# Zero rows for the 64-row operands of block attention on TensorE

## The chip, the cores and the metric

The kernel runs on one core of a Trainium2 chip. The metric is the device time of one execution in microseconds (us); less is better. Engines: TensorE (PE, with its weight loads PEld), VectorE (DVE), ScalarE (ACT), GpSimd (POOL) and the queue engine SyncE (SP).

## What is computed

Block-causal attention over 4 batches of 8 heads (576 tokens, head size 64), a mixture of experts (top 2 of 8) on the result, and a dense MLP behind it. The change lies in the attention:

```python
block = 64
scores = scale * np.matmul(q, k.transpose(0, 1, 3, 2))
pos = np.arange(S)                                   # S = 576
mask = (pos[:, None] // block) >= (pos[None, :] // block)
scores = np.where(mask, scores, -1000000000.0)
scores = scores - np.max(scores, axis=-1, keepdims=True)
attn = np.exp(scores)
attn = attn / (np.sum(attn, axis=-1, keepdims=True) + 1e-09)
return np.matmul(attn, v)                            # D = 64
```

`x = attention`, then `x = moe(x)` with 512 -> 1024 -> 512 per expert, then `mlp(x)` with 512 -> 2048 -> 512, all in float32.

## The kernel before

The program has three stretches: attention with the gating of each batch (to about 280 us), the experts, and the dense MLP.

Attention works head by head, 32 heads, a pair of heads per load. The 576 queries are cut into five chunks `QC`: the first has 64 queries, the others 128. The keys are cut from the other end: four chunks of 128 keys and a last one of 64. So a query chunk sees whole key blocks, chunk c sees 64 + 128c keys, and the mask falls into the last 64 keys of a chunk only. Numbers that need more than one pass of the array's precision are split in a high and a low part (`pth`, `ptl`; the V tile holds its high and low part side by side, 2 x 64 columns).

For each head and chunk these steps run:

- `scores` (L726): PE writes Q K^T into a PSUM tile `sb`; it works by units (0 and 1 together, 2, 3, 4).
- `rowmax` (L740) on DVE with a memset of the masked corner (L927), then `expo` (L747) on ACT, which writes P[c], one SBUF tile per query chunk with (c + 1) x 128 columns, and the row sums `rs`.
- `ptrans` (L765): PE transposes P[c] in pieces of 128 keys into a PSUM bank `tb`. P[0] has 64 rows, so its transpose takes 64 rows and a 64 x 64 piece of the identity. The piece (0, 1) is left out.
- `pt_hi` (L593, on ACT or DVE) and `pt_lo` (L784, DVE) write the transposed P into `pth` and `ptl`: key chunk kc at column kc x 576, keys on the partitions. Key chunk 4 has 64 keys and so fills 64 partitions, and only query chunk 4 (128 columns) sees it.
- `av` (L800): PE multiplies V with `pth` and `ptl`. Part 0 covers queries 0 to 319 with key chunks 0 to 2, part 1 queries 320 to 575 with key chunks 0 to 4. Where fewer than 256 columns remain, the product with `ptl` takes the 64 high columns of V alone. For key chunk 4 only the `nk` = 64 rows that exist are passed.
- `av_out`, `fin` (L822, PE: projects back to tokens and adds the gate's weights), `x_out` (DVE), `lsum` (POOL).

In the transposes P is the stationary operand (the weights) and the identity moves through; in the V products V is stationary and P moves.

The order of each engine's instructions comes from a planner (`Plan`): every operation gets a cost per engine, its dependencies, a priority and a PSUM bank, and is placed when engine, operands and bank would be free. The planned costs stand in the calls of `add`; the engines then run these fixed orders and wait for each other by semaphores. The constants of the phase are filled by POOL ahead of the loop (L613 to L626): zero rows of the raw inputs, the columns of P behind the visible keys, ones in `rs`. The V tile's rows 64 to 127 of key chunk 4 are zero from there.

Of the kernel before, what the change touches and what calls it, by code (L numbers as in the profile page):

```python
# [7 lines left out]
F32 = mybir.dt.float32  # L8
# [7 lines left out]
PSUM = bass.MemoryType.PSUM  # L16
# [20 lines left out]


class Bank:
    """A PSUM bank of a pool, held from the op that takes it until every op that drops it is done."""  # L40

    def __init__(self, pool, least):
        self.pool, self.least, self.left, self.bank, self.tile = pool, least, 0, None, None


class Plan:
    """Static list scheduling: each op is emitted when its engine, its operands and a PSUM bank would be free."""

    LAT = {"PE": 0.26, "DVE": 0.17, "ACT": 0.17, "POOL": 0.15, "SP": 2.0}
    OWN = {"PE": 0.0, "DVE": 0.13, "ACT": 0.13, "POOL": 0.1, "SP": 0.0}  # L50
# [81 lines left out]
def kernel(  # L132
# [14 lines left out]
    nc = tc.nc  # L147
    B, H, S, D = q.shape
# [24 lines left out]
    y_tab = tc.dram_tile([E * CAP + OVF * 128, DM], F32, name="y_tab")  # L173
# [24 lines left out]
    ident = const.tile([128, 128], F32, name="ident")  # L198
# [70 lines left out]
    slot = [const.tile([128, B, NC], I32, name=f"slot{i}") for i in range(2)]  # L269
# [137 lines left out]
        nc.vector.scalar_tensor_tensor(h[1][:, c0:c1], ps[:, :c1 - c0], 0.0, h[0][:, c0:c1].bitcast(F32),  # L407
                                       op0=OP.max, op1=OP.subtract)

# [1 line left out]
    gctx = ExitStack()  # L411
    sqk_p = gctx.enter_context(tc.tile_pool(name="sqk", bufs=2, side="right", reuse_waits="tile"))
    g_p = gctx.enter_context(tc.tile_pool(name="g", bufs=1, side="right", reuse_waits="tile"))
# [159 lines left out]
    with actx:  # L573
        pool = lambda name, bufs: actx.enter_context(tc.tile_pool(name=name, bufs=bufs))
# [11 lines left out]
        PW = S  # L586
# [23 lines left out]
        def dve(n):  # L610
            return {"DVE": 0.07 + n / 960.0}

        # constants of this phase  # L613
        for nm, pad in (("q", 0), ("k", NC - 1), ("v", NC - 1)):
            for i in range(2):
                if i or nm == "v":
# [1 line left out]
        P = []  # L618
        for c in range(NC):
            P.append(one.tile([128, (c + 1) * 128], F32, name=f"P{c}"))  # L620
            nc.gpsimd.memset(P[c][:, c * 128 + 64:], 0.0)
        rs = []
        for i in range(3):
            rs.append(one.tile([128, NC], F32, name=f"rs{i}"))
            nc.gpsimd.memset(rs[i][64:, 0:1], 1.0)
        pth = one.tile([128, 4 * PW + S], F32R, name="pth")  # L626
        ptl = one.tile([128, 4 * PW + S], F32R, name="ptl")

        def init_iw(e):
            for r in range(2):  # L630
                rows = slice(r * 64, (r + 1) * 64)
                for i, wo in enumerate((0, D)):
                    for j, src in enumerate((w_gate, w_noise)):
                        nc.sync.dma_start(iw[rows, :, i, wo + j * E:wo + (j + 1) * E],
                                          src.rearrange("(j i d) e -> i d j e", d=D, i=2)[i])
# [120 lines left out]
        def ptrans(g, i):  # L756
            ps = tb[g.bank]
            q0, n = PTQ[i]
            for c, kc in PT[i]:
                if (c, kc) == (0, 1):  # L760
                    continue
                s0, m = QC[c]
                o = (kc - PTK[i][0]) * n + s0 - q0
                nk = min(128, S - kc * 128)
                nc.tensor.transpose(ps[:nk, o:o + m], P[c][:m, kc * 128:kc * 128 + nk], ident[:m, :m])  # L765

        def pslice(t, i):
            k0, k1 = PTK[i]
# [20 lines left out]
        def av(g, hd, part):  # L789
            c0, c1 = PARTS[part]  # L790
            a, n = PQ[part]
            z = a + n
            vs = sp["v", hd // 2]
            o = tb[g.bank]
            for kc in range(c1):
                nk = min(128, S - 128 * kc)
                q0 = max(a, QC[kc][0])
                for ti, pp in enumerate((pth, ptl) if kc < c1 - 1 else (ptl, pth)):
                    w = D if pp is ptl and z - q0 < 256 else 2 * D
                    nc.tensor.matmul(o[:w, q0 - a:z - a], lhsT=vs[:nk, kc, hd % 2, :w],  # L800
                                     rhs=pp[:nk, kc * PW + q0:kc * PW + z],
                                     start=(kc == 0 and ti == 0), stop=(kc == c1 - 1 and ti == 1))

        def av_out(e, g, hd, part):
# [52 lines left out]
        for p in range(NPAIR):  # L857
            b, j = pairs[p]
            u0 = 2 * NU * p
            # operands of the pair  # L860
            for n_, nm in enumerate("qkv"):
                if p or nm == "v":
                    k["L", nm, p] = add({"SP": 1.6}, lambda e, p=p, nm=nm: load(p, nm),
# [49 lines left out]
            for hd in (2 * p, 2 * p + 1):  # L913
                i_ = hd % 2
                h = hd % H
                last = hd == HD - 1
# [82 lines left out]
            add({"DVE": 0.34}, lambda e, f=f, g=g: h_lo(hT["a", f], tb[g.bank], 0, AHEAD * 128), [hh], PR["es"] + f, drop=g)  # L999
        busy = plan.run({"POOL": 4.4, "DVE": 2.9, "PE": 4.4 + 0.216 * WARM0, "ACT": 2.0, "SP": 3.7})  # L1000

# [1 line left out]
    work = ctx.enter_context(tc.tile_pool(name="work", bufs=2, reuse_waits="tile"))  # L1003
    ps_h = ctx.enter_context(tc.tile_pool(name="ps_h", bufs=2, space=PSUM, reuse_waits="tile"))
    ps_y = ctx.enter_context(tc.tile_pool(name="ps_y", bufs=1, space=PSUM, reuse_waits="tile"))
# [74 lines left out]
    ovf = {}  # L1080

    def route_rows():
        """Rows of y_tab by token, and the list of slot tiles past the main capacity."""
        R = [128, 2 * NC, E]
        cps = ps_x.tile([128, E], F32, tag="x", name="cps")
        nc.tensor.matmul(cps, lhsT=ones, rhs=ohsum[B - 1], start=True, stop=True)
        cnt = work.tile([128, E], F32, tag="cnt", name="cnt", bufs=1)
        nc.vector.tensor_copy(cnt, cps)
        yield
        ge = work.tile([128, E, NV], F32, tag="ge", name="ge", bufs=1)  # L1090
        nc.vector.tensor_tensor(ge, cnt[:, :, None].to_broadcast([128, E, NV]),
                                tstart[:, None, :].to_broadcast([128, E, NV]), op=OP.is_gt)
        yield
        nt = work.tile([128, E], F32, tag="nt", name="nt", bufs=1)
        nc.vector.tensor_reduce(nt, ge, axis=AX.X, op=OP.add)
        yield
        cum = work.tile([128, E], F32, tag="cum", name="cum", bufs=1)
        nc.vector.tensor_tensor_scan(cum, one8, nt, 0.0, op0=OP.mult, op1=OP.add)
        yield
        off = work.tile([128, E], F32, tag="off", name="off", bufs=1)  # L1100
        nc.vector.tensor_tensor(off, cum, nt, op=OP.subtract)
        yield
        nc.vector.tensor_scalar(off, off, 128.0, float(E * CAP - MAIN), op0=OP.mult, op1=OP.add)
        yield
        nc.vector.tensor_tensor(off, off, erow, op=OP.subtract)
        yield
        for b in range(B):
            t = work.tile([128, 2 * NC, E], F32, tag="rt", name="rt", bufs=1)
            oh = ohs[b].rearrange("p i c e -> p (i c) e")
            pf = posi[b].rearrange("p i c -> p (i c)")  # L1110
            m = work.tile([128, 2, 2 * NC], F32, tag="rm", name="rm")
            for r, row in enumerate((erow, off)):
                nc.vector.tensor_tensor(t, oh, row[:, None, :].to_broadcast(R), op=OP.mult)
                yield
                nc.vector.tensor_reduce(m[:, r], t, axis=AX.X, op=OP.add)
                yield
            nc.vector.scalar_tensor_tensor(m[:, 1], pf, float(MAIN), m[:, 1], op0=OP.is_ge, op1=OP.mult)
            yield
            nc.vector.tensor_tensor(m[:, 0], m[:, 0], pf, op=OP.add)
            yield  # L1120
            nc.vector.tensor_tensor(m[:, 0], m[:, 0], m[:, 1], op=OP.add)
            yield
            for i in range(2):
                nc.vector.tensor_copy(slot[i][:, b], m[:, 0, i * NC:(i + 1) * NC])
                yield
        L = [128, OVF, E]
        le = work.tile([128, OVF, E], F32, tag="le", name="le", bufs=1)
        nc.vector.tensor_tensor(le, cum[:, None, :].to_broadcast(L), ovn[:, :, None].to_broadcast(L), op=OP.is_le)
        yield
        lst = const.tile([128, 2, OVF], F32, name="lst")  # L1130
        nc.vector.tensor_reduce(lst[:, 0], le, axis=AX.X, op=OP.add)
        yield
        nc.vector.tensor_tensor(le, le, nt[:, None, :].to_broadcast(L), op=OP.mult)
        yield
        nc.vector.tensor_reduce(lst[:, 1], le, axis=AX.X, op=OP.add)
        yield
        nc.vector.tensor_tensor(lst[:, 1], ovn, lst[:, 1], op=OP.subtract)
        yield
        nc.vector.tensor_scalar(lst[:, 1], lst[:, 1], 128.0, float(MAIN), op0=OP.mult, op1=OP.add)
        yield  # L1140
        nov = const.tile([128, 1 + OVF], I32, name="nov")
        nc.vector.tensor_copy(nov[:, 0:1], cum[:, E - 1:E])
        nc.vector.tensor_copy(nov[:, 1:], lst[:, 0])
        for i in range(2):
            for r in range(2):
                rows = slice(r * 64, (r + 1) * 64)
                nc.vector.tensor_copy(srd[i][rows], slot[i][0:64].rearrange("p (a r) c -> p r a c", r=2)[:, r, :, 0])
                nc.vector.tensor_copy(rrd[i][rows], rw[i][0:64].rearrange("p (a r) c -> p r a c", r=2)[:, r, :, 0])
                yield
        ovf["lst"], ovf["nov"] = lst, nov  # L1150
        yield 0
# [87 lines left out]
    def combined(gi, t):  # L1239
        x_tile(("m", gi), gath.pop((gi, t))[0][0], t, len(GR[gi]) * 128)  # L1240

    # the first tiles of expert 0 while the last tokens are routed
    plan2 = Plan({"h": 2, "x": 1, "y": NT - AHEAD})
    add = plan2.add
    k2 = {}
# [53 lines left out]
    wraw2[0] = ctx.enter_context(tc.tile_pool(name="wraw2", bufs=4, side="right", reuse_waits="tile"))  # L1299

    rr = route_rows()
    NG = len(STEPS)
    conv_at = [g for g in range(7, NG) if g % 3][:32]
# [40 lines left out]
        if NG - NF + 5 <= g < NG - NF + 5 + len(GR[0]):  # L1344
            combined(0, g - (NG - NF + 5))

# [1 line left out]
    def m_s1(i, gi, f):  # L1348
        n = len(GR[gi]) * 128
        ps = s1(("m", gi), f, U0 + i, 0, n, SP0 if gi == 0 else ())  # L1350
# [73 lines left out]
```

## Time and profile before

| | us |
|---|---|
| median of 3 runs | 1156.43 |
| range of the runs | 1153.89 to 1157.19 |
| profiled execution, span from its first to its last instruction | 1155.9 |
| PE busy in it | 1137.4 |
| DVE busy | 802.6 |
| ACT busy | 567.7 |
| POOL busy | 280.7 |

The page gives no other time for the profiled execution than its span; it lies 0.5 us below the median of the runs. In the timeline each row has a start, a length, engine, line, operation, tiles, and for PE the active rows and columns of the array as "rows*columns" ahead of the output's shape (partitions x elements). Equal neighbours are merged to one row with a count (x7), and the shape shown is that of the first. A matmul's recorded length holds its whole way through the array, so neighbours overlap; the distance of two starts tells what one operation took from PE. A group "rows*columns" of 64*128 is an operand with 64 rows.

### The profile page before, as it was taken

How to read it: one execution, taken by the hardware profiler on the slowest of the kernel's cores; microseconds unless marked ns; L12 is line 12 of the kernel's file. 1: busy time of each engine (PE TensorE's matmuls, PEld its weight loads, DVE VectorE, ACT ScalarE, POOL GpSimd, SP SyncE). 2: the span in 40 equal slices, each digit the busy share in tenths (PEclk: the TensorE clock that was granted, in tenths of full speed). 3: DMA queues.
4: the chain of work that ended last, by engine and by line, in shares of the span. 5: the costliest groups of instructions: out<-in, count | busy, mean ns of one | idle time of the engine just before them, and what ended most of it. 6: DMA issues, size and time to landing. Idle time of an engine off the chain costs nothing. (4 is left out here: it accounts for less than half of the span.)

```text
span 1155.9 us, 18249 instructions
## 1 busy us (share of the span) xinstructions
PE 1137.4 (98%) x6652; PEld 991.3 (86%) x6652; DVE 802.6 (69%) x1659; ACT 567.7 (49%) x1179; POOL 280.7 (24%) x299
## 2 busy tenths in 40 slices
PE   7999999999999999999999999899999999999998
PEld 5888889888898999999999999798888888888887
DVE  7888888888658878878778774577555564554543
ACT  5788787885443333333323233466444344443442
POOL 5545635443720101010100000176320230200000
PEclk9999999999999999999999999999999999999999
DMA  6754565221296785865564531522110110100000
GB/s 136 192 140 114 130 152 124 53 63 40 94 387 222 248 286 179 278 243 185 176 229 156 205 111 37 184 82 70 31 46 23 42 47 0 56 1 1 37 1 37
DMA packets 134340, 139.71 MB, mean 121 GB/s; under 512 B 67816, under 2 KB 97512, under 8 KB 134248
## 3 DMA queue, kind: packets, MB, share of 16 engines
q1 hardware_dynamic: 118568, 100.30, 27.6%
q0 software_dynamic: 8480, 28.78, 9.0%
q10 hardware_dynamic: 7200, 9.44, 2.3%
q8 instruction: 53, 0.87, 0.3%
q14 instruction: 39, 0.32, 0.1%
HBM read 92.94 MB, written 36.70 MB: 112 GB/s over the span
## 5 line engine op out<-in xcount | busy, mean ns | idle before, releaser
L381 PE MATMUL h<-xh,wah 128*128 128x312 f32 (+5 forms) x832 | 279.9, 336 | 2.9 <-DVE hl L407 2.8
L383 PE MATMUL h<-xh,wal 128*128 128x312 f32 (+5 forms) x832 | 275.1, 331 | 0.0
L382 PE MATMUL h<-xl,wah 128*128 128x312 f32 (+5 forms) x832 | 275.0, 331 | 0.0
L1060 PE MATMUL y<-wbh,hh 128*128 128x512 f32 (+1 forms) x608 | 238.2, 392 | 2.1 <-issue 2.1
L1061 PE MATMUL y<-wbl,hh 128*128 128x512 f32 (+1 forms) x608 | 238.7, 393 | 0.2
L1062 PE MATMUL y<-wbh,hl 128*128 128x512 f32 (+1 forms) x608 | 237.7, 391 | 0.0
L381 PEld LDWEIGHTS h<-xh,wah 128*128 128x128 f32 x832 | 157.6, 189 | 15.2 <-DVE hl L407 3.2
L382 PEld LDWEIGHTS h<-xl,wah 128*128 128x128 f32 x832 | 157.7, 190 | 11.5
L383 PEld LDWEIGHTS h<-xh,wal 128*128 128x128 f32 x832 | 157.4, 189 | 10.3
L1062 PEld LDWEIGHTS y<-wbh,hl 128*128 128x128 f32 (+1 forms) x608 | 113.7, 187 | 25.8
L1060 PEld LDWEIGHTS y<-wbh,hh 128*128 128x128 f32 (+1 forms) x608 | 113.8, 187 | 23.5 <-issue 2.6
L1061 PEld LDWEIGHTS y<-wbl,hh 128*128 128x128 f32 (+1 forms) x608 | 113.8, 187 | 22.3 <-POOL wbl L331 0.8
L404 ACT ACTIVATE hh<-h 128x312 fp32r<-128x312 f32 (+4 forms) x128 | 55.2, 431 | 145.7 <-PE h L383 144.2
L1353 DVE SCALAR_TENSOR_TENSOR r<-r,h 128x512 f32<-128x512 f32 (+1 forms) x80 | 50.5, 631 | 109.1 <-ACT r L1352 108.8
L1352 ACT ACTIVATE r<-h,three 128x512 f32<-128x512 f32 (+1 forms) x80 | 51.6, 645 | 126.9 <-PE h L383 126.7
L1224 POOL DMA_INDIRECT ga<-y_tab,slot x32 | 37.9, 1185 | 295.0 <-DMA wb<-w_out 114.4
L331 DVE TENSOR_TENSOR wal<-wa,wah 128x1024 fp32r<-128x1024 f32 x75 | 93.2, 1243 | 16.6 <-ACT wah L327 16.3
L1038 POOL DMA_INDIRECT xn<-x_tok,ids x38 | 38.9, 1024 | 269.4 <-PE xps L344 264.9
L747 ACT ACTIVATE P<-sb,nm 128x320 f32<-128x320 f32 (+4 forms) x160 | 84.8, 531 | 22.1 <-DVE nm L740 18.8
L331 DVE TENSOR_TENSOR wbl<-wb,wbh 128x1024 fp32r<-128x1024 f32 x71 | 86.5, 1218 | 12.9 <-ACT wbh L327 12.9
L347 ACT CAST xh<-xps 128x512 fp32r<-128x512 f32 x56 | 32.6, 586 | 126.7 <-PE xps L344 126.7
L1356 DVE TENSOR_TENSOR hl<-r,hh 128x512 fp32r<-128x512 f32 (+1 forms) x80 | 56.3, 703 | 51.5 <-ACT hh L1355 51.0
(236 smaller groups left out, 1990.2 us busy)
## 6 DMA issues: line engine op xcount, KB each, us to landing
wa<-in_moe_w_dram SPq DMA_DIRECT2D x23, 512.0 KB, 5.3
wb<-in_moe_w_dram SPq DMA_DIRECT2D x23, 512.0 KB, 8.5
qw<-qk POOLq DMA_DIRECT2D x30, 288.0 KB, 3.4
y_tab<-yo SPq DMA_DIRECT2D x32, 256.0 KB, 4.1
w<-in_moe_w_in_dram SPq DMA_DIRECT2D x16, 512.0 KB, 6.7
y_tab<-zero SPq DMA_DIRECT2D x8, 1024.0 KB, 9.9
w<-in_moe_w_out_dram SPq DMA_DIRECT2D x16, 512.0 KB, 5.6
wa<-in_moe_w_dram ACTq DMA_DIRECT2D x9, 512.0 KB, 9.5
```

The source lines that it names most:

```text
L331: (nc.gpsimd if e == "POOL" else nc.vector).tensor_tensor(lo, raws[PS[u]][which], hi.bitcast(F32), op=OP.subtract)
L381: nc.tensor.matmul(ps, lhsT=wh, rhs=xh, start=first, stop=False)
L382: nc.tensor.matmul(ps, lhsT=wh, rhs=xl, start=False, stop=False)
L383: nc.tensor.matmul(ps, lhsT=wl, rhs=xh, start=False, stop=last)
L404: nc.scalar.activation(h[0][:, c0:c1], ps[:, :c1 - c0], AF.Relu)
L747: nc.scalar.activation(o, views.pop((hd, c)), AF.Exp, bias=nms.pop((hd, c))[:n], scale=1.0, accum_out=rs[hd % 3][:n, c:c + 1])
L1060: nc.tensor.matmul(yps[t][:n], lhsT=hh[:, sl], rhs=wh[:, f % 2], start=first, stop=False)
L1061: nc.tensor.matmul(yps[t][:n], lhsT=hh[:, sl], rhs=wl[:, f % 2], start=False, stop=False)
L1062: nc.tensor.matmul(yps[t][:n], lhsT=hl[:, sl], rhs=wh[:, f % 2], start=False, stop=last)
L1352: nc.scalar.activation(r[:, :n], ps[:, :n], AF.Relu, bias=three, scale=1.0)
L1353: nc.vector.scalar_tensor_tensor(r[:, :n], r[:, :n], 6.0, ps[:, :n], op0=OP.min, op1=OP.mult)
L1356: nc.vector.tensor_tensor(hl[:, :n], r[:, :n], hh[:, :n].bitcast(F32), op=OP.subtract)
```

## The change

Three edits, all in attention. The transpose of P[0] is made with 128 rows and 128 moving columns (`ptrans`); for this P[0] is filled with zeros as a whole. The V products of key chunk 4 take 128 rows of `pth`, `ptl` and V; for this rows 64 to 127 of the last 128 columns of `pth` and `ptl` are filled with zeros once.

```diff
         for c in range(NC):
             P.append(one.tile([128, (c + 1) * 128], F32, name=f"P{c}"))
-            nc.gpsimd.memset(P[c][:, c * 128 + 64:], 0.0)
+            nc.gpsimd.memset(P[c] if c == 0 else P[c][:, c * 128 + 64:], 0.0)
...
         pth = one.tile([128, 4 * PW + S], F32R, name="pth")
         ptl = one.tile([128, 4 * PW + S], F32R, name="ptl")
+        for t in (pth, ptl):
+            nc.gpsimd.memset(t[64:, 4 * PW + S - 128:].bitcast(F32), 0.0)
...
                 nk = min(128, S - kc * 128)
-                nc.tensor.transpose(ps[:nk, o:o + m], P[c][:m, kc * 128:kc * 128 + nk], ident[:m, :m])
+                nc.tensor.transpose(ps[:nk, o:o + 128], P[c][:, kc * 128:kc * 128 + nk], ident)
...
             for kc in range(c1):
-                nk = min(128, S - 128 * kc)
                 q0 = max(a, QC[kc][0])
...
-                    nc.tensor.matmul(o[:w, q0 - a:z - a], lhsT=vs[:nk, kc, hd % 2, :w],
-                                     rhs=pp[:nk, kc * PW + q0:kc * PW + z],
+                    nc.tensor.matmul(o[:w, q0 - a:z - a], lhsT=vs[:, kc, hd % 2, :w],
+                                     rhs=pp[:, kc * PW + q0:kc * PW + z],
```

The rest of the diff takes comments and docstrings away. The planner's costs are as they were, so the order of instructions is the same on every engine but POOL, which has two more fills at the start. Line numbers behind the edits are 1 or 2 higher.

PE, one head in the middle of attention, around the transpose of P[0] (L765 before, L767 after; the shapes are those of the output). Before:

```order
L726 MATMUL sb_182<-qk 128x320
L726 MATMUL sb_182<-qk,qw 128x320
L765 MATMUL tb_176<-ident,P_187 128x64
L765 MATMUL tb_176<-ident,P_189 128x128 x2
L765 MATMUL tb_180<-ident,P_195 128x128 x4
```

And after:

```order
L728 MATMUL sb_182<-qk,qw 128x320
L767 MATMUL tb_176<-ident,P_187 128x128
L767 MATMUL tb_176<-ident,P_189 128x128 x2
L767 MATMUL tb_180<-ident,P_195 128x128 x4
L801 MATMUL tb_178<-pth,sp_v 128x256
```

Nothing has moved; the first transpose writes 128 columns instead of 64, of which the next one overwrites the upper 64.

POOL at its start, from the fill of P[0] to the first low part of V. Before:

```order
L621 MEMSET P_187 128x64
L621 MEMSET P_189 128x64
L621 MEMSET P_191 128x64
L621 MEMSET P_193 128x64
L621 MEMSET P_195 128x64
L625 MEMSET rs_197 64x1
L625 MEMSET rs_199 64x1
L625 MEMSET rs_201 64x1
L651 TENSOR_TENSOR sp_v<-raw_v_76,sp_v 128x10x64
```

And after:

```order
L621 MEMSET P_187 128x128
L621 MEMSET P_189 128x64
L621 MEMSET P_191 128x64
L621 MEMSET P_193 128x64
L621 MEMSET P_195 128x64
L625 MEMSET rs_197 64x1
L625 MEMSET rs_199 64x1
L625 MEMSET rs_201 64x1
L629 MEMSET pth 64x128
L629 MEMSET ptl 64x128
L653 TENSOR_TENSOR sp_v<-raw_v_76,sp_v 128x10x64
```

Two fills stand between the last `rs` and the first split, and the fill of P[0] is twice as wide. ACT's first exponential of a 64 x 64 tile waits for POOL in the new program, where it waited for DVE alone.

## Rows read from the trace of the kernel before

**Rows 1.** The page: busy time, share of the span, instructions of each engine.

```profile
PE 1137.4 (98%) x6652; PEld 991.3 (86%) x6652; DVE 802.6 (69%) x1659; ACT 567.7 (49%) x1179; POOL 280.7 (24%) x299
```

**Rows 2.** Busy time by stretch, 60 to 260 us: length, engines, clock; one and the sum.

```profile
140.00:180.00 40.00, 40.00 (x313) 36.05 (x312) 36.08 (x126) 31.66 (x99) 18.32 (x22) 1.00 0.56 137
...
sum 200.00, PE 199.84 PEld 179.11 DVE 171.30 ACT 162.32 POOL 96.26; mean PE 39.97 PEld 35.82 DVE 34.26 ACT 32.46 POOL 19.25
```

**Rows 3.** Waits of DVE, 60 to 260 us: total us, times, longest.

```profile
DVE sb L927 <- PE sb L726: 16.8, 31, 1.2
...
DVE x L830 <- PE tb L822: 2.3, 5, 0.5
```

**Rows 4.** Waits of PE over the whole span, longest first.

```profile
PE h L381 <- DVE hl L407: 2.8, 1, 2.8
PE sb L726 <- ACT P L747: 2.3, 2, 1.5
PE y L1060 <- issue: 2.1, 1, 2.1
...
PE tb L662 <- DVE sb L927: 1.6, 1, 1.6
```

**Rows 5.** Lines by form, PE: count | busy us, mean ns of one | idle before.

```profile
L800 PE MATMUL tb<-pth,sp_v 64*128 64x128 f32 x32 | 8.7, 272 | 0.0
L800 PE MATMUL tb<-ptl,sp_v 64*64 64x128 f32 x32 | 8.7, 271 | 0.0
L765 PE MATMUL tb<-ident,P 64*128 64x64 f32 x32 | 8.6, 268 | 0.0
```

**Rows 6.** Timeline of PE, end of a head's part 1: start us, length us.

```profile
102.81 0.48 PE L800 MATMUL tb<-ptl,sp_v 128*128 128x256 f32 x2
...
103.33 0.24 PE L726 MATMUL sb<-qk 128*64 128x64 f32 x1
...
103.47 0.34 PE L726 MATMUL sb<-qk 128*128 128x192 f32 x1
```

**Rows 7.** Timeline of PE, end of a head's part 0.

```profile
185.91 0.34 PE L800 MATMUL tb<-ptl,sp_v 128*128 128x256 f32 x2
186.08 0.27 PE L800 MATMUL tb<-pth,sp_v 128*128 128x128 f32 x1
186.19 0.20 PE L726 MATMUL sb<-qk 128*64 128x64 f32 x1
...
186.28 0.34 PE L726 MATMUL sb<-qk 128*128 128x192 f32 x1
```

**Rows 8.** Timeline of PE, transposes with P[0] ahead of the next scores.

```profile
256.25 0.30 PE L726 MATMUL sb<-qk,qw 128*128 128x320 f32 x1
256.48 0.64 PE L765 MATMUL tb<-ident,P 64*128 64x64 f32 x3
256.88 0.27 PE L726 MATMUL sb<-qk 128*64 128x64 f32 x1
```

**Rows 9.** Timeline of PE, transposes of 128 rows at such a place.

```profile
29.43 0.31 PE L726 MATMUL sb<-qk,qw 128*128 128x320 f32 x1
29.58 0.60 PE L765 MATMUL tb<-ident,P 128*128 128x128 f32 x4
29.93 0.27 PE L726 MATMUL sb<-qk 128*64 128x64 f32 x1
```

**Rows 10.** Timeline of POOL, its first split, with the idle time before it.

```profile
9.00 1.55 POOL L651 TENSOR_TENSOR sp_v<-raw_v,sp_v 128x640 fp32r<-128x640 f32 x1 [4.91 <-ACT sp_v L593]
```

**Rows 11.** Timeline of ACT, the first exponential of a 64 x 64 tile.

```profile
12.21 0.31 ACT L747 ACTIVATE P<-sb,nm 64x64 f32<-64x64 f32 x1
```

**Rows 12.** A stop of PE in head 1 (timeline), and the stretch behind it.

```profile
22.83 0.63 PE L662 MATMUL tb<-ident,sp_q 128*128 128x128 f32 x4 [1.58 <-DVE sb L927]
23.20:26.60 3.40, 3.40 (x17) 3.29 (x16) 2.25 (x7) 1.28 (x5) 1.15 (x1) 0.53 0.55 95
```

## The prediction

> **What bounds the kernel now.** I read the page's busy line first: TensorE (PE) is busy for 98% of the span [rows 1]. A busy PE may still be a PE that waits inside its pipeline, so the next views are stretches of the attention phase. From 60 to 260 us PE shows 199.84 of 200 us busy, VectorE (DVE) 171.30, ScalarE (ACT) 162.32, and in the fullest 40 us DVE has 36.08 [rows 2]. The list of waits has no row of PE in these 200 us, while DVE waits 16.8 us for PE's scores and 2.3 us for its projection [rows 3]. So in the middle of attention PE works through a fixed list, the others keep up, and an operation that PE gets rid of shortens the phase, as long as the others still keep up. Over the whole span PE's waits are few: 2.8 us just after attention, 2.3 and 1.6 us in the first two heads, one of 2.1 us late in the experts [rows 4]. Nothing behind attention holds PE for a time that would swallow a shift of the start.
>
> The changed operations are one transpose and two V products per head, 32 of each [rows 5]. They use 64 of the array's 128 rows (the first number of 64*128), nearly everything around them uses 128. A matmul's recorded length (about 270 ns) is mostly latency; what counts is the distance from start to start, so from here on I read the timeline only by its starts.
>
> **The V product's last chunk.** In the second part of a head, from the start of the last full 256-column product (102.81, merged with the first 64-row one) past the second 64-row product to the third operation behind (103.47) it takes 0.66 us; the first 64-row start is not shown apart, but the operation behind the pair starts at 103.33, 0.52 us after 102.81 [rows 6]. The first part of a head holds the same sequence with 128 rows: a 256-column product, a 128-column one with 64 weight columns, a 128-column one with 128, and then the same scores. There it goes 185.91, 186.19, 186.28: 0.28 us to the operation behind, 0.37 us to the third [rows 7]. The padded pair has exactly the shapes of this second sequence, so each head should save 0.66 - 0.37 = 0.29 us. The cost of 64 zero rows is in that figure already: it is nil, since the number of columns is the same.
>
> The Trainium skill, page "TensorEngine Tiling (Array Packing)", section "Key Properties", says that a change of tiling mode, not only of the tile, drains TensorE, and that page counts 64 rows and 64 columns alike as modes. For rows the trace agrees (0.52 against 0.28 us). For columns it doesn't: the product with 64 weight columns in the padded-like sequence starts and is followed without any such step, as the 0.17 us from 185.91 to 186.08 for two products show [rows 7]. By the page alone the 64-column weights would go on draining the array on either side after the change.
>
> **The first chunk's transpose.** It moves 64 columns now and 128 after. Before: from the last score product (256.25) to the transpose is 0.23 us, and it and the two behind it take 0.40 us until the next scores begin (256.48 to 256.88), 0.63 us in all [rows 8]. The same scores followed by four 128-row transposes and then by the same next scores: 0.15 us (29.43 to 29.58) and 0.35 us for four (29.58 to 29.93) [rows 9]. Three of those would be 0.35 x 3/4 = 0.26 us, and by the 0.11 us between 128-row products in [rows 7] taken off 0.35 it is 0.24; I take 0.24. After: 0.15 + 0.24 = 0.39 us, so 0.63 - 0.39 = 0.24 us saved, the 64 added moving columns included.
>
> **What else is added.** The zero fill of the first P tile becomes twice as wide, and two fills of 64 x 128 are new on GpSimd (POOL) at the start. POOL is idle for 4.91 us there until 9.00 us, because it waits for ACT and the loads [rows 10], so these cost nothing; bare they would be three short fills, under 1 us once (the idle time is the bound). ACT's first 64 x 64 exponential has a new wait for POOL's fill; it runs at 12.21 us [rows 11], more than 3 us after the fills must be over, and later heads have no wait of that kind. PE, DVE, ACT and SP keep their order, since the planner's costs are untouched; no DMA is added or moved. The added transposed columns are overwritten by the next transpose, in order on PE.
>
> **The sum on PE.** 32 x (0.29 + 0.24) = 17.0 us. Two places have the 64-row product directly before the 64-row transpose; they share one way in and one way out, so about half of their 0.53 us goes, and in one head the transpose lies behind other 64-row transposes that stay, so its 0.24 us goes: 17.0 - 0.5 - 0.24 = 16.2 us. The first two heads run with PE waiting 2.3 + 1.6 us for ACT and DVE [rows 4]; their 1.06 us go into those waits, which leaves 15.2.
>
> **What is late next.** In 60 to 260 us some 24 heads lie (32 in about 270 us), so PE would need 24 x 0.53 = 12.7 us less. DVE waits 16.8 + 2.3 = 19.1 us for PE there [rows 3], so on average it can follow: 200 - 19.1 = 180.9 us of its own against PE's 187.3. The margin is 6.4 us of 187, or 3%, and it is not even: the fullest 40 us have 36.08 us of DVE work [rows 2] against 40 - 2.5 = 37.5 us of PE. What PE waits for, P's low part and the exponentials, comes from there, and a head is only some 8 us long, so some heads will find DVE late. Bounds: nothing given back (DVE's average), or 6.4 us, if two engines that are nearly equal wait for each other alike and PE waits as long for DVE as DVE then still does for PE (19.1 - 12.7). I choose 2 us, nearer to nothing, because PE has no wait row at all in this stretch now. Forecast: 15.2 - 2 = 13 us. Against the profiled execution's span of 1155.9 us this is 1142.9; the median of the runs, 1156.43, is 0.5 us above the span, so I say 1143.4 us, 1.1% faster.
>
> **Rivals.** (1) DVE takes over: attention's last stretches are set by its queue and PE stalls on P's low part in most heads. For: 36.08 of 40 us busy. Against: it waits 19.1 us for PE today. Price: the 6.4 us of the bound above instead of 2, up to 10 if ACT, which is fed by DVE, comes late with it; a gain of 15.2 - 6.4 = 9 down to 5 us, about 8, so 1148 us. (2) The product with 64 weight columns begins to stall as the 64-row one does now, a step of about 0.1 us in and one out (0.24 / 2 each, from [rows 6, 7]). Then the V product saves 0.29 - 0.2 = 0.09 us, and the sum is 32 x (0.09 + 0.24) = 10.6, less 0.7 for the three odd heads, 0.7 for the first two and the 2 given back: 7.2 us, 1149 us. Against it stand the starts in [rows 7], where such a product passes without a stall. It is what the Trainium skill's page "TensorEngine Tiling (Array Packing)", "Key Properties", taken word for word, would give. (3) No change: the gap of 64-row operations isn't from the rows but from a wait on the same instruction, or the shift ends in the 2.8 us wait after attention [rows 4], because DVE's chain of the last heads ends as before: 1156 us, within 2. Against: no row of [rows 6, 8] carries an idle time with a releaser, and the first of the P[0] transposes and the V product wait for different things, yet both show the step. (4) Slower: PE runs ahead, meets DVE late, stands still for over a microsecond, and its clock drops. The trace has this in head 1: 1.58 us of idle before 22.83, and from 23.2 to 26.6 us a granted clock of 0.53 [rows 12], near the lower of its two levels (1.2 of 2.4 GHz), which costs 3.4 x 0.47 = 1.6 us more, so 3.2 us for each. It decides from five such stalls on (16 us eat the gain of 15.2); with seven, 22.4 - 15.2 = 7.2 us are lost and the time is 1164 us. Against: from 60 to 260 us PE waits in no row at all now, so it starts without one.
>
> **How the numbers follow.** Chances: forecast (gain 11 to 16 us) 0.64, rival 1 0.20, rival 2 0.03, rival 3 0.08, rival 4 0.05. About 3.5 us (0.3%) is what a measurement of this kernel can tell from no change, so faster has 0.64 + 0.20 + 0.03 = 0.87, same 0.08, slower 0.05. The range goes from 1139.5 (16.2 us and the noise of the runs) up to 1150.0, which takes in rivals 1 and 2 for the most part and leaves out some 0.18.
>
> **What would show it.** In the changed kernel the timeline should have the P transposes 0.11 us apart with no 0.2 us step at the first, and the last V product followed after about 0.28 us as in [rows 7]; if these steps stay, the cause isn't the rows. The lines by form should have no 64*128 entries at these two lines, and the first expert's products should begin about 13 us earlier than now. If the steps go but the time doesn't, the list of waits should have new rows of PE on DVE's low part of P or on ACT's exponentials, and DVE's waits for the scores should be gone; that would be rival 1. A lower granted clock in the middle slices would be rival 4.

## The result

The changed kernel takes 1143.34 us in the median of 4 runs (1142.37 to 1144.68), the kernel before 1156.51 us beside it (4 runs); the ratio is 0.9893, 95% interval 0.9875 to 0.9910. In a second series, beside the experiments, it took 1141.53 us against 1155.49, ratio 0.9883 (0.9869 to 0.9897). The profiled execution has a span of 1142.9 us, 13.0 us less than the 1155.9 of before.

The page's busy line of the changed kernel, the counterpart of [rows 1], shows PE 14.6 us less busy and the other engines as they were:

```profile
PE 1122.8 (98%) x6652; PEld 988.6 (87%) x6652; DVE 803.7 (70%) x1659; ACT 565.9 (50%) x1179; POOL 282.7 (25%) x301
```

The lines by form ([rows 5]) have lost the 64*128 and 64*64 operands at these two lines; the V products and the transposes are in the groups of full height now (416 + 32 transposes, 32 + 32 of either V product):

```profile
L767 PE MATMUL tb<-ident,P 128*128 128x128 f32 x448 | 67.1, 275 | 0.6 <-DVE ptl L786 0.6
...
L801 PE MATMUL tb<-pth,sp_v 128*128 128x128 f32 x64 | 17.6, 275 | 0.0
L801 PE MATMUL tb<-ptl,sp_v 128*64 128x128 f32 x64 | 14.2, 221 | 0.0
```

The timeline of PE in one head of the changed kernel, read by the starts in the first column as in [rows 6] and [rows 8]:

```profile
97.25 0.31 PE L728 MATMUL sb<-qk,qw 128*128 128x320 f32 x1
97.40 0.93 PE L767 MATMUL tb<-ident,P 128*128 128x128 f32 x7
98.08 0.36 PE L801 MATMUL tb<-pth,sp_v 128*128 128x256 f32 x1
...
99.00 0.34 PE L801 MATMUL tb<-ptl,sp_v 128*128 128x256 f32 x2
99.17 0.27 PE L801 MATMUL tb<-pth,sp_v 128*128 128x128 f32 x1
99.28 0.20 PE L728 MATMUL sb<-qk 128*64 128x64 f32 x1
...
99.37 0.34 PE L728 MATMUL sb<-qk 128*128 128x192 f32 x1
```

The scores are followed by the first transpose after 0.15 us (0.23 before), seven transposes take 0.68 us, 0.10 each, and the end of the V product takes 0.28 us to the next scores (0.52 before) and 0.37 us to the third operation (0.66 before): the figures of [rows 7] and [rows 9] to the hundredth.

Where the 13 us came from is seen in three places of the timeline. Before, with head 2's first 64 x 64 scores at 29.93 in [rows 9], head 31's scores and the first product of the experts:

```profile
266.07 0.24 PE L726 MATMUL sb<-qk 128*64 128x64 f32 x1
...
278.92 0.36 PE L381 MATMUL h<-xh,wah 128*128 128x256 f32 x1
```

and the same three after:

```profile
29.79 0.27 PE L728 MATMUL sb<-qk 128*64 128x64 f32 x1
...
253.56 0.20 PE L728 MATMUL sb<-qk 128*64 128x64 f32 x1
...
265.83 0.36 PE L381 MATMUL h<-xh,wah 128*128 128x256 f32 x1
```

Up to head 2 the change gains 0.14 us, from there to head 31 12.4 us, to the first expert 13.1 us in all, and from there to the end both take the same (877.0 and 877.1 us). PE's order is the same in both kernels, so its products can be laid side by side one by one, and the differences of the distances from start to start added up by place (heads 2 to 30 in the three middle rows):

| place | after, us | second profile of after, us |
|---|---|---|
| before head 2 | -0.14 | -0.34 |
| V product of the last chunk and the four products behind | -8.44 | -8.46 |
| transpose of P[0], the way in and the two behind | -6.11 | -6.66 |
| all other products of PE | +2.18 | +2.03 |
| head 31 to the first expert | -0.56 | -0.56 |
| sum | -13.07 | -13.99 |

The waits of PE between 28 and 265 us name the larger part of the row +2: 1.9 us (1.5 in the second profile), where the kernel before has one row, 0.3 us:

```profile
PE tb L801 <- DVE ptl L786: 1.3, 2, 0.7
PE tb L767 <- DVE ptl L786: 0.6, 2, 0.4
```

DVE, the counterpart of [rows 2] and [rows 3] for 60 to 260 us, is busy for 181.61 instead of 171.30 us, and its waits for the scores have gone from 16.8 to 9.3 us:

```profile
sum 200.00, PE 198.70 PEld 186.75 DVE 181.61 ACT 168.51 POOL 97.95; mean PE 39.74 PEld 37.35 DVE 36.32 ACT 33.70 POOL 19.59
```

```profile
DVE sb L928 <- PE sb L728: 9.3, 24, 0.8
...
DVE x L831 <- PE tb L823: 1.7, 4, 0.5
```

### The profile page after: what moved, and what is told of

It reads as the page before. It is cut to its first block, busy times and chain, and to the rows that moved or that the text cites. A ratio compares the mean times of both kernels' runs of the same rounds, so it can differ in the third digit from the quotient of the medians.

```text
span 1142.9 us, 18252 instructions
## 1 busy us (share of the span) xinstructions
PE 1122.8 (98%) x6652; PEld 988.6 (87%) x6652; DVE 803.7 (70%) x1659; ACT 565.9 (50%) x1179; POOL 282.7 (25%) x301
```

## The experiments

The theory: an operand of 64 rows costs PE a step on the way in and on the way out, because the array changes between 64 and 128 rows; it costs this wherever it stands; PE bounds attention, so the steps are paid in full, but for some 2 us, since DVE comes late more often once PE is faster. The rivals: the steps belong to something else at these two places, to the 64 weight columns, or the gain is limited by DVE whichever step goes. All times are medians, the ratio is against the kernel before in the same series. What "the changed kernel" took beside them is 1141.5 us (the series with it) and 1143.3 us (the first).

**The two halves alone.** In the first the transpose stays as it was (and with it the fill of P[0]):

```diff
-                nc.tensor.transpose(ps[:nk, o:o + 128], P[c][:, kc * 128:kc * 128 + nk], ident)
+                nc.tensor.transpose(ps[:nk, o:o + m], P[c][:m, kc * 128:kc * 128 + nk], ident[:m, :m])
```

> Only the V product of the last key chunk has 128 rows; the transpose of P[0] keeps 64. Theory (each step between 64 and 128 rows costs PE about 0.1 us or more, and PE bounds attention): 32 x 0.29 us, less some 0.4 for two places beside the 64-row transpose, 0.6 for the first two heads and under 1 given back: 7.5 to 8.5 us faster than before, 1148 to 1149 us; the timeline shows 0.28 us behind the last full product. Rival (DVE is the bound as soon as PE gets faster): the same 4 to 5 us whichever half is done. Rival (the 64 weight columns stall instead): 2 to 3 us.

1148.12 us, ratio 0.9940 (0.9927 to 0.9952), 7.4 us faster than before. Its timeline shows one step gone and the other in its place: 0.24 us from the scores to the first transpose, 0.83 us for the seven, 0.28 us behind the V product.

```profile
98.48 0.30 PE L728 MATMUL sb<-qk,qw 128*128 128x320 f32 x1
98.72 1.07 PE L767 MATMUL tb<-ident,P 64*128 64x64 f32 x7
99.55 0.36 PE L801 MATMUL tb<-pth,sp_v 128*128 128x256 f32 x1
...
100.47 0.34 PE L801 MATMUL tb<-ptl,sp_v 128*128 128x256 f32 x2
...
100.75 0.20 PE L728 MATMUL sb<-qk 128*64 128x64 f32 x1
```

In the second the V product stays as it was (with `nk` rows, no fills of `pth` and `ptl`):

```diff
-                    nc.tensor.matmul(o[:w, q0 - a:z - a], lhsT=vs[:, kc, hd % 2, :w],
-                                     rhs=pp[:, kc * PW + q0:kc * PW + z],
+                    nc.tensor.matmul(o[:w, q0 - a:z - a], lhsT=vs[:nk, kc, hd % 2, :w],
+                                     rhs=pp[:nk, kc * PW + q0:kc * PW + z],
```

> Only the transpose of P[0] has 128 rows and 128 moving columns; the V product keeps 64 rows. Theory: 32 x 0.24 us, less 0.5 for the places where the 64-row product or transposes lie beside it, 0.5 for the first two heads and under 1 given back: 5.5 to 6.5 us faster, 1150 to 1151 us. The two halves alone together give 13 to 15 us, a little more than both at once, if some is given back only when PE gains most. Rival (the transpose's step belongs to the change from scores to transposes and not to the rows): within 1.5 us of before.

1149.74 us, ratio 0.9951 (0.9939 to 0.9963), 5.8 us faster. Its V product still takes 0.52 us to the next scores:

```profile
99.87 0.48 PE L800 MATMUL tb<-ptl,sp_v 128*128 128x256 f32 x2
...
100.39 0.24 PE L726 MATMUL sb<-qk 128*64 128x64 f32 x1
```

The halves add up to 13.1 us, both at once gave 13.2 and 14.0. So neither hides the other, and the rival that DVE cuts off the gain at 4 to 5 us is gone. The totals hold a start that differs from profile to profile by some 1.5 us (last section); heads 2 to 30 alone don't. By the same adding up as in the table above, those of the first half gained 7.87 us at the V product and lost 0.83 elsewhere, those of the second gained 6.11 us at the transpose and 0.35 at the V product, and lost 0.81. That is 7.0 + 5.7 = 12.7 us net, against 12.4 and 13.1 in the two profiles of both at once. The losses of 0.8 + 0.8 are a little less than the 2.0 to 2.2 of both together.

The changed kernel beside them:

> The changed kernel once more, as the mark for the other runs beside it: 1143.3 us, 13 us under the kernel before (ratio 0.988 to 0.990).

1141.53 us, ratio 0.9883; the 1143.3 of the first series lies 1.8 us higher, which is the size of what two series differ by.

**One more visit to 64 rows, where there was none.** Ahead of the transposes of query chunk 4 the first of them is made once more, from 64 rows, and in a second kernel from 128:

```diff
+                if i == 3 and kc == 0:
+                    nc.tensor.transpose(ps[:, o:o + 64], P[c][:64, 0:128], ident[:64, :64])
```

```diff
+                if i == 3 and kc == 0:
+                    nc.tensor.transpose(ps[:, o:o + 128], P[c][:, 0:128], ident)
```

> The changed kernel with one more transpose per head at another place: ahead of the four transposes of query chunk 4, the first of them is made once more from 64 rows only (64 columns, overwritten by the next). Theory (the step belongs to the rows, wherever it stands): about 0.1 us on the way in, 0.2 us for the operation and the way out, 0.06 us behind, some 0.35 us per head or 11 us, of which 1 to 2 come back because PE then waits less: 9 to 11 us slower than the changed kernel, 1151 to 1153 us. Rival (the step came from the places, P[0] and the last key chunk): no more than the next kernel, 3 us.

> The changed kernel with the same additional transpose from all 128 rows. Theory: 0.11 us per head, 3.5 us on PE, some of it hidden in waits: 2 to 3.5 us slower than the changed kernel, 1144 to 1146 us. The difference to the kernel with the 64-row one, 6 to 8 us, is the price of one visit to 64 rows per head, taken at a place that neither kernel had.

The first took 1148.80 us, ratio 0.9944 (0.9931 to 0.9958), the second 1142.23 us, ratio 0.9889 (0.9874 to 0.9904): 6.6 us between them. The timelines, first with 64 rows, then with 128:

```profile
106.97 0.49 PE L769 MATMUL tb<-ident,P 128*128 128x128 f32 x3
107.39 0.27 PE L768 MATMUL tb<-ident,P 64*128 64x64 f32 x1
107.59 0.66 PE L769 MATMUL tb<-ident,P 128*128 128x128 f32 x4
108.00 0.36 PE L803 MATMUL tb<-pth,sp_v 128*128 128x256 f32 x1
```

```profile
104.08 0.49 PE L769 MATMUL tb<-ident,P 128*128 128x128 f32 x3
104.40 0.27 PE L768 MATMUL tb<-ident,P 128*128 128x128 f32 x1
104.51 0.60 PE L769 MATMUL tb<-ident,P 128*128 128x128 f32 x4
104.87 0.36 PE L803 MATMUL tb<-pth,sp_v 128*128 128x256 f32 x1
```

From the first row's start to the last it is 1.03 us with 64 rows and 0.79 with 128; the three ahead take 0.42 against 0.32, the operation itself 0.20 against 0.11, the four behind 0.41 against 0.36. These neighbours are transposes of the same kind on the same tile, and no row carries an idle time, so neither the change from scores to transposes nor a wait is left as a cause: a visit to 64 rows costs 0.24 us here too. The transposes of 64 rows also move 64 columns instead of 128; the 64-row V products move 128 like the padded ones, and have the step all the same.

What the step looks like is seen at the weight loads (PEld), first with 64 rows, then with 128:

```profile
107.39 0.13 PEld L768 LDWEIGHTS tb<-ident,P 64*128 64x128 f32 x1 [0.17 <-issue]
```

```profile
104.30 0.14 PEld L768 LDWEIGHTS tb<-ident,P 128*128 128x128 f32 x1
```

With 128 rows the load begins 0.10 us ahead of its transpose (104.40), beside the one before it. With 64 rows it begins together with its transpose (107.39), after 0.17 us in which the load engine waits for nothing that the profile shows. So at the change of rows the load isn't laid beside the product ahead. Whether the array has to run empty first, or something else holds the load, the trace doesn't tell.

From the first scores of head 2 to those of head 31 it took 231.5 us with 64 rows and 226.1 with 128 (223.1 and 223.8 in the two profiles of the changed kernel), 5.5 us between them and 2.3 to 3.0 us for the plain one. My totals were too high: the one with 64 rows lost 5.5 to 7.3 us against the changed kernel (by which series of it) and not 9 to 11, the plain one -1.1 to 0.7 and not 2 to 3.5. The profiles tell of two things beside the transposes. From the first expert's product on both take 873.3 us, against 877.1 and 874.9 in the two profiles of the changed kernel; and in the plain one head 2 begins at 27.99 us instead of 29.79, which the last section takes up.

**The 64-row transposes that are left.** Q and K of a pair have a run of four of them in `prep`:

```diff
-                    nc.tensor.transpose(ps[:, i * BLK:(i + 1) * BLK], sq[:BLK, 0, i, :], ident[:BLK, :BLK])
-                    nc.tensor.transpose(ps[:, (2 + i) * BLK:(3 + i) * BLK], sk[:BLK, NC - 1, i, :], ident[:BLK, :BLK])
+                for i in range(4):
+                    src = sq[:, 0, i, :] if i < 2 else sk[:, NC - 1, i - 2, :]
+                    nc.tensor.transpose(ps[:, i * BLK:i * BLK + 128], src, ident)
```

> The changed kernel, and the four 64-row transposes of each pair's Q and K (16 runs of four) made with 128 rows and 128 columns too. By starts in the timeline a run of four with its way in and out takes some 0.59 us now, and four at 0.11 us with the 0.2 us that lie between a transpose and the projection anyway would take about 0.64: the way in and out is shared by four, and inside the run a 64-row transpose takes only 0.06 us. So 0 to 1 us slower than the changed kernel, 1143 to 1144.5 us. Rival (every run of 64-row operands costs 0.24 us): 16 x 0.24 = 3.8 us faster, 1139.5 us.

1142.55 us, ratio 0.9887 (0.9873 to 0.9901): 1.0 us over the changed kernel beside it, inside the interval, and not 3.8 us faster. The run in the changed kernel, from the four transposes ahead of it to the projection behind:

```profile
110.00 0.60 PE L767 MATMUL tb<-ident,P 128*128 128x128 f32 x4
110.53 0.27 PE L667 MATMUL tb<-ident,sp_q 64*128 64x64 f32 x1
...
110.92 1.40 PE L823 MATMUL tb<-iw,oT 128*64 128x80 f32 x10
```

takes 0.92 us, and with 128 rows

```profile
109.28 0.60 PE L767 MATMUL tb<-ident,P 128*128 128x128 f32 x4
109.71 0.38 PE L668 MATMUL tb<-ident,sp_q 128*128 128x128 f32 x2
109.93 0.38 PE L668 MATMUL tb<-ident,sp_k 128*128 128x128 f32 x2
110.24 1.40 PE L823 MATMUL tb<-iw,oT 128*64 128x80 f32 x10
```

0.96 us. So padding is not good in itself. A run of several 64-row operations pays the way in and out once, and inside it they come faster than padded ones (single starts at 110.53, 110.64, 110.70 and 110.76, against 0.11 us each). And the padded run doesn't get rid of the step at its end: the projection's first product, with 64 weight columns, begins 0.20 us after a transpose of 128 rows too, and its load has the same idle time ahead of it:

```profile
110.24 0.47 PEld L823 LDWEIGHTS tb<-iw,oT 128*64 128x64 f32 x3 [0.17 <-issue]
```

Ahead of another operation of 128 rows the result could be another one. An estimate from the starts above: with a way out of 0.20 us and 0.05 behind it, as in the kernel with the additional 64-row transpose, it would be 0.69 us from the last transpose ahead of the run (110.33) to the operation behind it, and five starts at 0.11 take 0.55. No run tests that.

**The 64 weight columns.** The low-part product takes all 128 weight columns:

```diff
-                    w = D if pp is ptl and z - q0 < 256 else 2 * D
+                    w = 2 * D
```

> The changed kernel, with the low-part product of each part's last key chunk taking all 128 weight columns instead of 64 (64 such products). Theory (64 columns cost no step): the product takes the 0.11 us of a 128-column weight instead of 0.06, so up to 64 x 0.05 = 3.2 us of PE more, 1144 to 1147 us. Rival (a change of columns drains the array as a change of rows does): faster than the changed kernel, by up to 64 x 0.1 us, under 1141 us.

1142.87 us, ratio 0.9882 (0.9866 to 0.9897): the same as the changed kernel within the interval. In its timeline the end of the V product takes 0.30 us (99.34 to 99.64) instead of 0.28, so there was no step of columns to be saved here, and the wider weights cost some 0.02 us and not the 0.05 that I had put down: their load begins at 99.34 with the product ahead.

```profile
99.34 0.34 PE L801 MATMUL tb<-ptl,sp_v 128*128 128x256 f32 x2
99.52 0.28 PE L801 MATMUL tb<-pth,sp_v 128*128 128x128 f32 x1
99.64 0.20 PE L728 MATMUL sb<-qk 128*64 128x64 f32 x1
```

That isn't so of every product with 64 columns. The projection's two come first of its ten, and in the second kernel of "Other orders" they stand behind scores in some heads:

```profile
103.75 0.31 PE L728 MATMUL sb<-qk,qw 128*128 128x320 f32 x1
103.99 1.40 PE L823 MATMUL tb<-iw,oT 128*64 128x80 f32 x10
```

These are 0.24 us, as much as from the same scores to a 64-row transpose ([rows 8], 0.23), and not the 0.15 to a 128-row one. Inside the projection the start of the first product with 128 columns lies 0.16 us behind the last with 64, the next is 0.17 behind that, and from there on they are 0.11 apart. The projection's operands are plain float32, those of the V product float32r; no run changes its columns or its type, so what makes this step is open.

**A lighter DVE.** The memset of the masked corner is left out, in the changed kernel and in the one before:

```diff
-                            ms = add({"DVE": 0.075}, lambda e, hd=hd, c=c: nc.vector.memset(tails.pop((hd, c)), NEG), [ms],
+                            ms = add({"DVE": 0.075}, lambda e, hd=hd, c=c: tails.pop((hd, c)), [ms],
```

> The changed kernel without DVE's memset of the masked corner (four per head, about 0.1 us each, so the masked scores are left in); the order of all else is the same. If the 2 to 3 us that PE lost again in attention are waits for DVE's queue, which is 91% busy now, a lighter DVE gives part of it back: 1 to 3 us faster than the changed kernel, 1140.5 to 1142.5 us, and PE's waits for the low part of P become fewer. Rival (they are lost at the start or to ACT): within 0.7 us of the changed kernel.

> The kernel before without the same memsets. There PE bounds attention and DVE waits 19 us for it, so a lighter DVE brings less than in the changed kernel: 0 to 1 us, within 0.1% of before. Rival (DVE is part of the bound in both): as much as in the changed kernel, 1 to 3 us.

1142.53 us (ratio 0.9881, 0.9866 to 0.9896) and 1156.31 us (ratio 1.0001, 0.9992 to 1.0010). The first total misses what I expected, it is no faster than the changed kernel. The attention itself is: the first expert's product starts at 261.96 us (265.83 and 264.93 in the two profiles of the changed kernel) and at 276.35 (278.92 before). Some 1.5 us of either lie ahead of head 2, which begins at 28.10 and 28.43 us; from head 2 to head 31 it is 221.6 us instead of 223.8 and 223.1, and 235.1 instead of 236.1. But both kernels need some 878.8 us from the first expert's product on, more than any other kernel here (873.3 to 877.1); without the mask the attention's output is another one and so, presumably, is what the experts get. So their totals aren't compared with the rest, and only the attention is read. In heads 2 to 30 the row "all other products", which is +2.18 and +2.03 us from the kernel before to the changed one, is +1.31 from one maskless kernel to the other (-0.76 and +0.55 against before). So some 0.8 us of the 2 go with a lighter DVE, by one profile of each maskless kernel. The one wait row that stays in the changed one from 28 to 260 us is that of the V product for `ptl`, 1.3 us, the first of the two rows in the result. DVE is a cause of the new waits, then, but some 0.4 us less of DVE work per head (four memsets of 0.11 us) doesn't remove them all. What the rest waits for is open.

**Other orders.** In the first kernel the planner may put the high-part casts of Q and K on ACT, in the second it is told of the cheaper PE steps (only the values that change in the line of `PR` are shown):

```diff
-'qa': False
+'qa': True
```

```diff
-'dav': (0.67, 1.02)
+'dav': (0.67, 0.85)
...
-'dpt': (0.27, 0.33, 0.44, 0.44, 0.11)
+'dpt': (0.18, 0.33, 0.44, 0.44, 0.11)
```

> The changed kernel, with the planner free to put the high-part casts of Q and K (0.48 us each, two per pair) on ACT instead of DVE, which moves part of the order on PE, DVE and ACT. If the 2 us that PE lost again are DVE's lateness, 0 to 2 us faster than the changed kernel; if ACT is as late as DVE, or the new order is worse, 0 to 3 us slower.

> The changed kernel with the planner told of the gain: the planned cost of the second V product falls from 1.02 to 0.85 us and that of the first transposes from 0.27 to 0.18. The order changes on PE, DVE and ACT. If an order made for the slower PE is what costs the 2 us of new waits, 0 to 2 us faster than the changed kernel; otherwise the same within 1 us, or slower if the new order meets other waits.

1144.92 us, ratio 0.9913 (0.9898 to 0.9928), and 1149.90 us, ratio 0.9947 (0.9933 to 0.9961): 3.4 and 8.4 us slower than the changed kernel in its better series, 1.6 and 6.6 than in the first. In both, PE waits in attention for DVE and for ACT in more places than in the changed kernel (28 to 262 us, second kernel, two of four rows):

```profile
PE tb L801 <- DVE ptl L786: 1.3, 5, 0.3
PE sb L728 <- ACT P L749: 0.7, 2, 0.5
...
```

The rows of the second add up to 3.1 us, 1.2 more than in the changed kernel, while its heads 2 to 30 take 7.4 to 8.1 us more, so most of its loss lies in no wait row; I haven't followed it. Neither order wins the 2 us back. That shows that the order made for the slower PE is as good as the first and better than the second, not that it has no part in the 2 us.

**The clock at the start.** Six products of constants fill PE's stop near 10.7 us:

```diff
+        for dep in (k["S", 0, 0],):
+            g = Bank("t", 1)
+
+            def fill(e, g=g):
+                for _ in range(6):
+                    nc.tensor.matmul(tb[g.bank], lhsT=ones, rhs=filler, start=True, stop=True)
+
+            add({"PE": 0.0001}, fill, [dep], -5000, take=g, drop=g)
```

> The changed kernel with six short products of constants on PE in the stop of some 1.6 us near 10.7 us, where PE waits for the first exponentials; nothing else is moved. In the profile of the changed kernel the granted clock is 0.50 from 12.8 to 16 us, and head 2 begins at 29.8 us; in profiles whose clock stays at 1.00 there, it begins at 28.0 to 28.5. Theory (the stop lets the clock fall, and that costs the start 1 to 2 us): clock 1.00 from 12.8 to 16 us, head 2 at 28 to 29 us, the whole 0.5 to 2 us faster than the changed kernel, 1140 to 1142.5 us. Rival (the slower clock there is hidden behind the waits of the first heads): head 2 within 0.3 us of 29.8, no gain.

1144.45 us, ratio 0.9898 (0.9882 to 0.9913), no gain. The stretch 12.8 to 16 us of the changed kernel, then of the filled one (engines' busy time, then the granted clock):

```profile
12.80:16.00 3.20, 3.20 (x15) 3.15 (x15) 3.09 (x10) 1.70 (x5) 1.75 (x2) 0.50 0.75 170
```

```profile
12.80:16.00 3.20, 3.20 (x28) 2.84 (x27) 3.09 (x10) 1.83 (x5) 1.75 (x2) 1.00 0.74 169
```

The clock is held at its upper level there, and head 2 still begins at 29.67 us. The rival was right: PE stops again ahead of 22.9 us, for DVE, and begins behind this stop at 22.98 us in the changed kernel and at 22.93 in the filled one, whatever it did before:

```profile
22.98 1.08 PE L664 MATMUL tb<-ident,sp_q 128*128 128x128 f32 x4 [1.59 <-DVE sb L928]
```

```profile
22.93 1.09 PE L664 MATMUL tb<-ident,sp_q 128*128 128x128 f32 x4 [1.58 <-DVE sb L928]
```

## Why the prediction was right

The forecast was 1143.4 us, a span of 1142.9, and both were met. Point by point:

- **V product, 0.29 us per head.** The table gives 8.44 / 29 = 0.29. The sequence of [rows 7], at full height in the same kernel, was the price of the changed one.
- **Transpose, 0.24 us per head, odd heads less.** The table gives 0.21 and 0.23 per head with the odd ones in it, the visit added at another place 0.24.
- **The first two heads' gain is lost.** 0.14 to 0.34 us of 1.06 came through. The reason is sharper than the one I gave: PE is released at 22.6 to 23.1 us by DVE in every kernel with the mask, so what PE saves before that point ends in this one wait. That head 2 begins within 0.34 us in both kernels' profiles is luck beside it: the granted clock behind the stop alone moves it by 1.5 us (last section).
- **2 us given back.** 2.0 to 2.2. That DVE has a part in it is shown by the waits on P's low part (1.9 us against 0.3) and by the maskless pair; that it is all of it was argued and isn't shown. The 2 itself was a choice between 0 and 6.4.
- **Nothing behind attention takes the shift away.** 877.0 and 877.1 us from the first expert's product on; the 2.8 us wait for the first experts stayed as it was.
- **Rival 1** (DVE takes over) would have shown up as halves that don't add up; they do. DVE still waits 9.3 + 1.7 = 11 us for PE from 60 to 260 us, more than the 6.4 I had left it. **Rival 2** (columns) fell with the 128-column weights. The page "TensorEngine Tiling (Array Packing)" of the Trainium skill says in "Key Properties" that a change of mode drains the array. For 64 and 128 rows the step that every run here shows fits (0.24 us per visit). For 64 and 128 columns the V product shows no step (0.28 against 0.30 us) and the projection shows one (0.24 against 0.15 us behind scores), so my reading in the prediction that columns don't count holds for the V product only. **Rival 3** fell with the additional visit. **Rival 4** didn't come: no stop of over 0.7 us from 28 us to the end of attention.

The total hit closer than it had a right to. The 0.5 us that I put between span and median come from one profiled execution; that of the changed kernel took 1144.68 us with its span of 1142.9, 1.3 above the median. The series differ by 1.8 us, and what lies behind the first expert's product differs from profile to profile, 873.3 to 877.1 us in those with the right mask, without any relation to the change.

## What to carry to other kernels

Price an operand by the distance from its start to the next start, and look for the same shape at full height in the same kernel: it gives the saving and the cost in one number. Where PE bounds the stage, as here, a lone 64-row operation or pair among 128-row ones is worth padding with zeros: 0.2 to 0.3 us at each of the places tried. A run of four, with the projection behind it, wasn't. Look at what stands behind the operation before you count its way out as saved. Before adding up such savings, cut off what lies ahead of the last point at which another engine releases PE.

## What the runs showed that I had not expected

PE's stop near 22.8 us lasts 1.57 to 1.60 us in the profiles with the mask, and yet the granted clock behind it (23.2 to 26.6 us) is 0.52 to 0.62 in some, near the lower of its two levels, and 1.00 in others, here the half with only the transposes changed:

```profile
23.20:26.60 3.40, 3.40 (x28) 3.17 (x27) 3.35 (x10) 2.56 (x9) 1.26 (x1) 1.00 0.51 84
```

and the changed kernel:

```profile
23.20:26.60 3.40, 3.40 (x17) 3.37 (x17) 2.39 (x7) 1.28 (x5) 1.28 (x1) 0.55 0.42 59
```

Where it stays at 1.00, head 2 begins at 28.0 to 28.5 us, otherwise at 29.6 to 30.0: some 1.5 us of the total hang on it. The kernel before ([rows 12]) and the changed one both have the lower clock in their profiles, so it isn't in their difference. The half with only the transposes changed and the kernel with the additional 128-row transpose have the upper one, which is a part of why the latter's total is as low as the changed kernel's. What decides it is open. The clock's fall near 12.8 us cost nothing that the filled kernel's profile shows.
